# Attention units in stretches of two: regrouping a fused retention and feed-forward kernel

## The chip, the cores and the metric

The kernel runs on one core of a Trainium2 chip. A core has five engines that run beside each other and wait for each other by semaphores: TensorE (matmuls; the profile shows them as PE and the loading of weights as PEld), VectorE (DVE), ScalarE (ACT), GpSimd (POOL) and SyncE (SP), which here only issues DMAs. Matmul results land in PSUM, which the program divides into eight buffers of 128 partitions and 512 float32 columns. The metric is the device time of one execution in microseconds, as the median of several; lower is better.

## The reference

A retention layer (attention without softmax, with a decay for each head) is followed by a feed-forward layer with an ELU between its two products:

```python
B, H, S, D_ = q.shape                       # 8, 8, 576, 64
scores = (1 / sqrt(D_)) * q @ k^T
gamma = 1.0 - 2.0 ** (-5.0 - arange(H))
rel = pos[:, None] - pos[None, :]
Dmat = where(rel >= 0, gamma ** rel, 0.0)   # for each head
attn = (scores * Dmat) @ v
x = attn.transpose(0, 2, 1, 3).reshape(4608, 512)
h = x @ w_in                                # 512 x 2048
g = where(h > 0, h, exp(min(h, 0)) - 1)
out = g @ w_out                             # 2048 x 512, float32
```

## The kernel before, in words

**The decay as a scaling.** gamma^(i-j) is split into a factor on the rows of q and one on the rows of k (tiles `gq`, `gk`, `far_q`, `far_k`), so that a causal mask of ones and zeros is all that is left to do on the scores. Past chunks enter through a state, the sum of k^T v over the tokens before.

**Units.** Each batch has 512 tokens that are worked in blocks of 256 and a tail of 64. A *unit* is 256 tokens of one batch (half T = 0 or 1) for four heads (w = 0 or 1); eight batches give 32 units, numbered 0 to 31 in the order (batch, T, w). The tails of four batches form one tail item, t0 and t1 (numbers 32 and 33). For each unit q, k and v are loaded (`load_main`, line 380), scaled (`scaled`) and v is cast; q and k are then turned, by TensorE for units 0 to 6 and by a transpose DMA on SP from unit 7 on.

**Two forms.** A unit before `FAR` (line 211) is worked in two chunks of 128 tokens: it is loaded with one DMA for each of q, k and v, has one mask over 1024 columns, two running states (`mid`, `end`) and two block-diagonal copies of them (`s_mid`, `s_end`) for the matmuls. From `FAR` = 8 on, a unit is worked in four chunks of 64 tokens: two DMAs for each of q, k and v, half the columns in the scores and the mask, four running states and four block-diagonal copies. The running states are made by VectorE one after the other (`after_state` line 733, `after_far` line 789), the block-diagonal copies by POOL as a rule.

**A stretch.** TensorE does attention work in *stretches* (`stretch`, line 914). A stretch serves two units at once: the outputs of the one before (`do_inter`, old states times queries; `do_values`, masked scores times v) and the scores and the states of the present one (`do_scores`, `do_state`). The inter matmuls use the full array, those of scores, values and states work in quarters of it, 64 by 64. The scores go to the `sc` buffer (1024 columns), and the mask on VectorE makes `pt` of them. Outputs and states share two of the six PSUM buffers called `f`: columns 0 to 255 hold outputs, the rest states. ScalarE or VectorE copies the outputs to `xt`, two copies a unit (`put_x`, line 867). The tail items have scores, values and inter matmuls, but no states of their own.

**The feed-forward** fills TensorE between the stretches. The first product (`ffn1`, line 977) makes 512 columns in one `f` buffer from four matmuls; ScalarE takes the exponential (`e`), VectorE makes `em` (or ScalarE a relu in place) and the activation `g`. The second product (`ffn2`, line 1033) adds up 16 matmuls of 512 columns in an `f` buffer, in steps of four; ScalarE copies the result to `ot`, and SP writes it out, in one DMA for 128 rows or, where `HALVED` (line 217) names the block and its part, in two of 64 rows.

**What sets the order.** Nothing is ordered by hand. Every step is an `Op` with an engine, a cost, what it needs, the buffers that it takes and a rank, and `Plan.run` (line 68) plays the engines through with these costs and picks on each engine the step of lowest rank that can start. The instructions are then issued in this order, and on the chip each engine works through its own list in order. A changed cost, such as those of the tail loads (`load_tail`, line 426) and of their transposes (`prepare_tail`, line 567), thus changes the order, and so do a buffer's number of places in `SLOTS` (line 225: six `f`, one `sc`, two raw tail tiles `rqt`, eight `s_mid`). A stretch takes its `f` buffers through `reserve` (line 905).

Of the kernel before, what the change touches and what calls it, by code (L numbers as in the profile page):

```python
# [17 lines left out]
P = 128  # L18
# [192 lines left out]
FAR = 8  # L211
FAR_LD = 0.64
# [4 lines left out]
HALVED = ((10, 1), (10, 2), (12, 0), (12, 1), (12, 2))  # L217
# [16 lines left out]
def kernel(  # L234
# [191 lines left out]
    def load_tail(it):  # L426
# [140 lines left out]
    def prepare_tail(it):  # L567
# [3 lines left out]
        for m in range(2):  # L571
            for j in range(2):
# [14 lines left out]
                def emit_t(op, m=m, j=j):  # L587
# [5 lines left out]
                                     dma=(1.0, 32)))  # L593
# [24 lines left out]
    def far_pt(n):  # L618
        return tiles["pt", n].rearrange("p i h n -> p (i h n)")[:, : 8 * C].rearrange("p (x n) -> p x n", n=C)

    def do_scores(it):
        n = it.n
        sc = tiles["sc", n]
# [12 lines left out]
        if it.far:  # L636
            for x in range(4):
                for i in range(2):
                    r = slice(i * D, (i + 1) * D)
                    for c in range(2):  # L640
                        cs = slice(c * C, (c + 1) * C)
                        mm(sc[cs, i, x * C : (x + 1) * C], tt[r, 4 + x, cs], tt[r, x, cs], start=True, stop=True)
# [11 lines left out]
    def do_inter(it, xkey):  # L654
# [10 lines left out]
        if it.far:  # L665
            tt = tiles["qkT", n]
            for x in range(4):
# [4 lines left out]
                for hl in range(2):  # L672
                    acc((xkey, c), 0, 2, tiles[xkey, c][:, hl * P + e * C : hl * P + (e + 1) * C], s[:, hl],
# [11 lines left out]
    def do_values(it, xkey):  # L685
# [12 lines left out]
        vn, pt = tiles["vn", n], tiles["pt", n]  # L698
        if it.far:
            pt = far_pt(n)  # L700
            for hl in range(2):
                for e in range(2):
                    for c in range(2):
                        cs = slice(c * C, (c + 1) * C)
                        o = hl * P + e * C
                        for i in range(2):
                            acc((xkey, c), 0, i, tiles[xkey, c][i * D : (i + 1) * D, o : o + C], vn[cs, 2 * hl + i, e],
                                pt[cs, 4 * i + 2 * e + hl])
# [24 lines left out]
    def after_state(it, st, views, bank_keys):  # L733
# [3 lines left out]
        if it.far:  # L737
            return after_far(it, st, views, bank_keys, prev)

# [3 lines left out]
        def emit_mid(op):  # L743
            dst = tiles["mid", n]
            if prev is None:
                pin(copy[op.eng](dst, st_ap(0)))
            else:
                pin(nc.vector.tensor_tensor(dst, st_ap(0), tiles[prev[1]], ALU.add))

        mid = add(f"mid{n}", {"DVE": 0.29} if it.T else {"DVE": 0.29, "ACT": (0.3, 0.2)}, [st, prev and prev[0]],  # L750
                  emit_mid, it.rank + 2, take=[T("mid", ("mid", n), [P, 2, D], FP32)],
                  use=[views[0][0]] + ([prev[1]] if prev else []), banks=[bank_keys[0]])

        def emit_end(op):
            pin(nc.vector.tensor_tensor(tiles["end", n], st_ap(1), tiles["mid", n], ALU.add))

        end = add(f"end{n}", {"DVE": 0.29}, [mid], emit_end, it.rank + 3,
                  take=[T("end", ("end", n), [P, 2, D], FP32)], use=[views[1][0], ("mid", n)], banks=[bank_keys[1]])
        total[it.w] = (end, ("end", n))

        def block(src, key, name, dep):
            def emit(op):
                pin(alu[op.eng].tensor_tensor(
                    tiles[key].rearrange("p h (j d) -> p h j d", j=2),
                    tiles[src].unsqueeze(2).to_broadcast([P, 2, 2, D]),
# [23 lines left out]
    def after_far(it, st, views, bank_keys, prev):  # L789

        n = it.n
        it.bms = []
        for x in range(4):
# [4 lines left out]
            def emit(op, c=c, e=e, key=key, prev=prev):  # L798
                new = views[c][2]()[:, e * P : (e + 1) * P].rearrange("p (h d) -> p h d", h=2)
                if prev is None:  # L800
                    pin(copy[op.eng](tiles[key], new))
                else:
                    pin(nc.vector.tensor_tensor(tiles[key], new, tiles[prev[1]], ALU.add))  # L803

            run = add(f"{key[0]}{x}_{n}", {"DVE": 0.29} if prev else {"DVE": 0.29, "ACT": (0.3, 0.2)},
                      [st, prev and prev[0]], emit, it.rank + 2, take=[T(key[0], key, [P, 2, D], FP32)],
                      use=[views[c][0]] + ([prev[1]] if prev else []), banks=[bank_keys[c]])
            prev = run, key
            out = (name, it.b, it.T, it.w) + ((x + 1,) if x < 3 else ())

            def emit_b(op, key=key, out=out):
                pin(alu[op.eng].tensor_tensor(  # L812
                    tiles[out].rearrange("p h (j d) -> p h j d", j=2),
                    tiles[key].unsqueeze(2).to_broadcast([P, 2, 2, D]),
                    diag.unsqueeze(1).unsqueeze(3).to_broadcast([P, 2, 2, D]), ALU.mult,
                ))

            blk = add(f"b{x}_{n}", {"POOL": 0.62, "DVE": (0.42, 1.5)}, [run], emit_b, it.rank + 3,
                      take=[T(name, out, [P, 2, P], BF16)], use=[key])
            if x < 3:  # L820
                it.bms.append(blk)
            else:
                it.be = blk
        total[it.w] = prev

    def mask_step(it, sc):
        n = it.n
        def emit(op):
            if it.tail:
                pin(nc.vector.tensor_tensor(  # L830
                    tiles["pt", n].rearrange("p i h n -> p (i h n)").rearrange("p (x n) -> p x n", n=ST),
                    tiles["sc", n].rearrange("p i n -> p (i n)").rearrange("p (x n) -> p x n", n=ST),
# [3 lines left out]
            if it.far:  # L836
                pin(nc.vector.tensor_tensor(  # L837
                    far_pt(n).rearrange("p (i x) n -> p i x n", i=2),
                    tiles["sc", n][:, :, : 4 * C].rearrange("p i (x n) -> p i x n", n=C),
                    mask_t.unsqueeze(1).unsqueeze(2).to_broadcast([P, 2, 4, C]), ALU.mult,  # L840
# [4 lines left out]
                tiles["sc", n].rearrange("p i (h n) -> p (i h) n", h=2),  # L845
# [3 lines left out]
        it.mask = add(f"mask{n}", {"DVE": 0.69 if it.far else 1.22}, [sc], emit, it.rank + 1,  # L849
                      take=[T("pt", ("pt", n), [P, 2, 2, 2 * P], BF16)], use=[("sc", n)], banks=[("sc", 0)])  # L850
# [366 lines left out]
```

## Time and profile before

| | |
|---|---|
| median of 3 runs | 304.0 us (303.87 to 304.51) |
| the profiled execution | 305.64 us, span 303.9 us |
| granted TensorE clock | 1.00 throughout |
| busy: PE, DVE, ACT, POOL | 291.6, 214.2, 155.2, 178.4 us |
| DMA | 50.13 MB; the mean busy share of the 16 engines is 0.8 to 1.2 up to 200 us, 0.1 to 0.2 after 240 us |
| end of the last unit's attention / of the second tail | 218 us / 237 us, only feed-forward from then on |
| mean time of: exp on ACT, copy of 512 columns on ACT, g on DVE | 0.597, 0.587, 0.68 us |

The span runs from the first to the last instruction of the core; the execution's own time has some 1.7 us around it. In the rows that follow, "out<-in" names the tiles, a shape is partitions x elements, and a matmul's "64*64" or "128*128" is the part of the array that it uses. A timeline row gives start, length, engine, line and how many instructions it merges; in square brackets stands the idle time of the engine before it and what ended it. The length of a matmul's row has a modelled end, so distances between starts are the better measure.

### The profile page before, as it was taken

What the parts mean: (1) busy time and instruction counts of PE and PEld (TensorE: products, weight loads), DVE (VectorE), ACT (ScalarE), POOL (GpSimd) and SP (SyncE); (2) the same over time, 40 slices, a digit from 0 to 9 for tenths busy, and PEclk for the clock granted to TensorE, in tenths of its full rate; (3) what the DMA queues carried; (4) which work ended last, traced back from release to release, by engine and by line L of the source; (5) the groups of instructions that cost most, each with busy time, mean ns of one, the idle gap of its engine ahead of it and who ended that gap; (6) DMA issues with size and microseconds to landing.
All of it is one profiled execution on the core that took longest, in us unless ns stands there. A gap on an engine that the chain in (4) does not pass through costs nothing.

```text
span 303.9 us, 8654 instructions
## 1 busy us (share of the span) xinstructions
PE 291.6 (96%) x3378; PEld 169.6 (56%) x3418; DVE 214.2 (70%) x436; ACT 155.2 (51%) x305; POOL 178.4 (59%) x300
## 2 busy tenths in 40 slices
PE   8889999999999999999999999999997999999995
PEld 4768746767666754445554544545444544444444
DVE  5878935958877857996988897788871486666500
ACT  2439724748655546765855544445541583444311
POOL 5880389688989897889889889697532000000000
PEclk9999999999999999999999999999999999999999
DMA  7999998999899999989999999987667101011132
GB/s 206 270 206 210 235 303 218 173 218 187 194 193 232 214 185 204 206 193 183 193 188 224 204 186 199 204 169 171 137 130 168 37 2 36 35 36 37 43 97 71
DMA packets 142010, 50.13 MB, mean 165 GB/s; under 512 B 120720, under 2 KB 137488, under 8 KB 141968
## 3 DMA queue, kind: packets, MB, share of 16 engines
q1 hardware_dynamic: 137744, 45.37, 71.4%
q0 software_dynamic: 4224, 4.19, 8.3%
q8 instruction: 27, 0.44, 0.6%
q14 instruction: 15, 0.12, 0.1%
HBM read 36.70 MB, written 9.44 MB: 152 GB/s over the span
## 4 chain that ended last, share of the span: by engine, by line
PE 85%; DMA 6%; DVE 3%; issue 2%; SPq 1%; POOL 1%; ACT 1%; POOLq 0%; DVEq 0%; ACTq 0%
PE f L268 82%; PE sc L268 3%; DMA rv<-in_v_dram 3%; DMA rqk<-in_q_dram 2%; DMA rqt<-in_k_dram 1%; DVE em L1010 1%; DVE g L1020 1%; DMA qkTt<-qkt 1%; DVE g L1018 1%; SPq L404 1%; PE f L523 0%; ACT e L996 0%; POOL qkn L475 0%; POOL qkt L578 0%; DVE mid L803 0%
## 5 line engine op out<-in xcount | busy, mean ns | idle before, releaser
L268 PE MATMUL f<-xt,w_in_sb 128*128 128x256 bf16 (+1 forms) x755 | 139.8, 325 | 0.8 <-DVE xt L882 0.2
L268 PE MATMUL f<-w_out_sb,g 128*128 128x512 bf16 (+2 forms) x581 | 137.2, 367 | 3.4 <-issue 1.7
L996 ACT ACTIVATE e<-f 128x512 f32<-128x512 f32 x144 | 85.4, 597 | 77.7 <-PE f L268 73.5
L268 PEld LDWEIGHTS <-w_in_sb 128*128 128x128 bf16 x768 | 73.7, 98 | 52.0 <-DVE xt L882 0.5
L268 PEld LDWEIGHTS <-g 128*128 128x128 bf16 x608 | 56.5, 98 | 59.2 <-issue 1.0
L1010 DVE TENSOR_SCALAR em<-e 128x512 bf16<-128x512 f32 x88 | 49.2, 560 | 35.3 <-ACT e L996 34.7
L1020 DVE SCALAR_TENSOR_TENSOR g<-f,em 128x512 bf16<-128x512 f32 x88 | 60.4, 689 | 5.5 <-DVE em L1010 0.5
L812 POOL TENSOR_TENSOR s_mid<-mid,diag 128x256 bf16<-128x256 f32 x72 | 44.5, 630 | 15.1 <-DVE mid L803 9.5
L1018 DVE SCALAR_TENSOR_TENSOR g<-e,f 128x512 bf16<-128x512 f32 x56 | 37.6, 681 | 2.5 <-ACT f L1006 2.1
L1054 ACT COPY ot<-f 128x512 f32<-128x512 f32 (+2 forms) x37 | 20.8, 564 | 28.4 <-PE f L268 25.5
L475 POOL TENSOR_TENSOR qkn<-rqk,far_q 128x256 bf16<-128x256 f32 x48 | 31.0, 658 | 1.8 <-DMA rqk<-in_q_dram 1.6
L475 POOL TENSOR_TENSOR qkn<-rqk,far_k 128x256 bf16<-128x256 f32 x48 | 31.0, 660 | 0.0
L1006 ACT ACTIVATE f<-f 128x512 f32<-128x512 f32 x51 | 30.1, 594 | 0.0
L882 ACT CAST xt<-f 128x256 bf16<-128x256 f32 x52 | 18.1, 390 | 20.8 <-PE f L268 20.2
L510 POOL CAST vn<-rv 128x512 bf16<-128x512 f32 x28 | 18.2, 651 | 6.2 <-DMA rv<-in_v_dram 6.1
L837 DVE TENSOR_TENSOR pt<-sc,mask_t 128x512 bf16<-128x512 f32 x24 | 16.4, 681 | 5.9 <-PE sc L268 5.9
L803 DVE TENSOR_TENSOR mid<-f,mid 128x128 f32<-128x128 f32 x48 | 13.8, 288 | 3.5
L578 POOL TENSOR_TENSOR qkt<-rqt,gq 128x256 bf16<-128x256 f32 x16 | 10.1, 652 | 10.3 <-DMA rqt<-in_k_dram 10.2
L812 POOL TENSOR_TENSOR s_end<-end,diag 128x256 bf16<-128x256 f32 x24 | 15.6, 648 | 0.1
L475 POOL TENSOR_TENSOR qkn<-rqk,gq 128x256 bf16<-128x256 f32 x13 | 8.3, 648 | 12.0 <-DMA rqk<-in_q_dram 11.9
L843 DVE TENSOR_TENSOR pt<-sc,mask 128x1024 bf16<-128x1024 f32 x8 | 9.7, 1219 | 2.1 <-PE sc L268 2.0
L268 PE MATMUL sc<-qkT 64*64 64x64 bf16 (+1 forms) x512 | 11.0, 204 | 0.0
(83 smaller groups left out, 177.8 us busy)
## 6 DMA issues: line engine op xcount, KB each, us to landing
out_dram<-ot SPq DMA_DIRECT2D x26, 256.0 KB, 2.9
rqk<-in_q_dram SPq DMA_DIRECT2D x48, 128.0 KB, 3.4
rqk<-in_k_dram SPq DMA_DIRECT2D x48, 128.0 KB, 3.4
rv<-in_v_dram SPq DMA_DIRECT2D x48, 128.0 KB, 3.4
out_dram<-ot SPq DMA_DIRECT2D x19, 128.0 KB, 2.4
rqk<-in_q_dram SPq DMA_DIRECT2D x8, 256.0 KB, 6.1
rqk<-in_k_dram SPq DMA_DIRECT2D x8, 256.0 KB, 5.8
rv<-in_v_dram SPq DMA_DIRECT2D x8, 256.0 KB, 6.0
```

The source lines that it names most:

```text
L268: pin(nc.tensor.matmul(*a, **kw))
L475: pin(alu[op.eng].tensor_tensor(tiles[key][:, i, e], tiles[raw][:, :, e], g, ALU.mult))
L510: pin(copy[op.eng](tiles["vn", n], tiles["rv", n]))
L812: pin(alu[op.eng].tensor_tensor(tiles[out].rearrange("p h (j d) -> p h j d", j=2), tiles[key].unsqueeze(2).to_broadcast([P, 2, 2, D]), dia ...
L837: pin(nc.vector.tensor_tensor(far_pt(n).rearrange("p (i x) n -> p i x n", i=2), tiles["sc", n][:, :, : 4 * C].rearrange("p i (x n) -> p i ...
L882: pin(copy[op.eng](dst, src))
L996: pin(nc.scalar.activation(tiles[ekey], tiles[hkey], AF.Exp))
L1006: pin(nc.scalar.activation(ph, ph, AF.Relu))
L1010: pin(alu[op.eng].tensor_scalar_add(em, e, -1.0))
L1018: pin(nc.vector.scalar_tensor_tensor(g, e, -1.0, ph, ALU.add, ALU.min))
L1020: pin(nc.vector.scalar_tensor_tensor(g, ph, 0.0, tiles["em", blk, p], ALU.max, ALU.min))
L1054: pin(copy[op.eng](tiles[okey][:, :cols], tiles[pkey][:, :cols]))
```

## The change

Four things change.

- `FAR` goes from 8 to 12: units 8 to 11 are worked in the 128-token form, like the units before them.
- From unit 16 (`PAIR`) on, a stretch takes two units, those of the two head groups of the same batch and half. Their scores share one `sc` buffer and one mask; their states go to two `f` buffers of their own, so that one addition serves both units; their outputs fill two further `f` buffers, and one copy serves both units (`put_two`). The tiles of the running states become twice as wide.
- The planner's costs of the tail loads (issue 0.46 to 0.63, transfer 0.8 to 0.93) and of their transposes (1.0 to 1.3) are raised, and that of a 64-token load goes from 0.64 to 0.62.
- Only part (12, 1) of the output is still written in halves, where there were five parts.

In the order of instructions that results, TensorE has 32 groups of attention matmuls between feed-forward work where it had 40; SP issues 256 DMAs where it issued 272. Between the first and the second tail stretch stand 68 feed-forward matmuls of 512 columns where there were 60, and ahead of the first tail stretch 52 where there were 32.

```diff
-FAR = 8
-FAR_LD = 0.64
+PAIR = 16
+FAR = 12
+FAR_LD = 0.62
-HALVED = ((10, 1), (10, 2), (12, 0), (12, 1), (12, 2))
+HALVED = ((12, 1),)
...
-            chain[0] = add(name, {"SP": 0.46}, [], emit, len(plan.ops),
+            chain[0] = add(name, {"SP": 0.63}, [], emit, len(plan.ops),
...
-                           dma=(0.8, 32), after=chain.get(0))
+                           dma=(0.93, 32), after=chain.get(0))
...
-                                     dma=(1.0, 32)))
+                                     dma=(1.3, 32)))
...
+    def after_far(its, st, view, bank_keys):
+        b, t, n, m = its[0].b, its[0].T, its[0].n, len(its)
+        prev = total.get(its[0].w) if t else None
...
             def emit(op, c=c, e=e, key=key, prev=prev):
-                new = views[c][2]()[:, e * P : (e + 1) * P].rearrange("p (h d) -> p h d", h=2)
+                new, dst = view(c, e), tiles[key].rearrange("p w h d -> p w (h d)")[:, :m]
                 if prev is None:
-                    pin(copy[op.eng](tiles[key], new))
+                    pin(copy[op.eng](dst, new))
                 else:
-                    pin(nc.vector.tensor_tensor(tiles[key], new, tiles[prev[1]], ALU.add))
...
+                    pin(nc.vector.tensor_tensor(dst, new, tiles[prev[1]].rearrange("p w h d -> p w (h d)")[:, :m], ALU.add))
...
             if it.far:
+                w = 4 if it.two_of is None else 8
                 pin(nc.vector.tensor_tensor(
...
-                    mask_t.unsqueeze(1).unsqueeze(2).to_broadcast([P, 2, 4, C]), ALU.mult,
+                    mask_t.unsqueeze(1).unsqueeze(2).to_broadcast([P, 2, w, C]), ALU.mult,
...
+    def put_two(its, xkey, dep):
+        for c in range(2):
+            it = its[0]
+            def emit(op, c=c, it=it):
+                dst = tiles[it.xt][:, :, it.T * TB : (it.T + 1) * TB].rearrange("p h (e c r) -> p c h e r", e=2, c=2)[:, c]
+                pin(copy[op.eng](dst, tiles[xkey, c].rearrange("p (h e r) -> p h e r", e=2, r=C)))
...
-    def stretch(prev, it):
-        xkey = ("x", it.n if it else "last")
+    def stretch(prevs, its):
+        name = str(its[0].n) if its else "last"
+        apart = len(prevs) > 1 or len(its) > 1
+        xkey = ("x", name)
+        skey = ("s", name) if apart else xkey
...
         def emit(op):
-            if prev is not None:
-                do_inter(prev, xkey)
-            if it is not None:
+            for i, it in enumerate(prevs):
+                do_inter(it, xkey, *([i * 2 * P] if len(prevs) > 1 else []))
+            for it in its:
                 do_scores(it)
-            if prev is not None:
-                do_values(prev, xkey)
-            if it is not None and not it.tail:
-                do_state(it, views)
+            for i, it in enumerate(prevs):
+                do_values(it, xkey, *([i * 2 * P] if len(prevs) > 1 else []))
+            if states:
+                for it in its:
+                    do_state(it, view_of(it))
...
-        reserve(st, [(xkey, c) for c in range(2)])
+        reserve(st, ([(xkey, c) for c in range(2)] if prevs or not apart else []) +
+                ([(skey, c) for c in range(2)] if apart and states else []))
...
-    prev = None
-    for it in items[EARLY:]:
-        stretch(prev, it)
-        prev = it
-    stretch(prev, None)
+    prev, left = [], items[EARLY:]
+    while prev or left:
+        now = left[: 2 if left and left[0].far and left[0].n >= PAIR else 1]
+        left = left[len(now) :]
+        stretch(prev, now)
+        prev = now
```

More of the change, by code (lines that the diff above doesn't have):

```diff
@@ L808, in after_far @@
-            prev = run, key
[L809 to L824, printed above, removed]
+                    pin(nc.vector.tensor_tensor(dst, new, tiles[prev[1]].rearrange("p w h d -> p w (h d)")[:, :m], ALU.add))
+            t0 = 0.29 if m == 1 else 0.42
+            run = add(f"{key[0]}{x}_{n}", {"DVE": t0} if prev else {"DVE": t0, "ACT": (t0 + 0.02, 0.2)},
+                      [st, prev and prev[0]], emit, its[0].rank + 2, take=[T(key[0], key, [P, 2, 2, D], FP32)],
+                      use=[bank_keys[c]] + ([prev[1]] if prev else []), banks=[(bank_keys[c], 0)])
@@ new lines, in after_far, with emit_b @@
+            prev = run, key
+            for i, it in enumerate(its):
+                out = (name, b, t, it.w) + ((x + 1,) if x < 3 else ())
+                def emit_b(op, key=key, out=out, i=i):
+                    pin(alu[op.eng].tensor_tensor(
+                        tiles[out].rearrange("p h (j d) -> p h j d", j=2),
+                        tiles[key][:, i].unsqueeze(2).to_broadcast([P, 2, 2, D]),
+                        diag.unsqueeze(1).unsqueeze(3).to_broadcast([P, 2, 2, D]), ALU.mult,
+                    ))
+                blk = add(f"b{x}_{it.n}", {"POOL": 0.62, "DVE": (0.42, 1.5)}, [run], emit_b, it.rank + 3,
+                          take=[T(name, out, [P, 2, P], BF16)], use=[key])
+                if x < 3:
+                    it.bms.append(blk)
+                else:
+                    it.be = blk
@@ L929, in emit, with view_of @@
+        if its:
+            take.append(T("sc", its[0].sc, [P, 2, 512], FP32))
+        states = bool(its) and not its[0].tail
+        def view_of(it):
+            o = 0 if apart else 2 * P
+            o += it.w * 2 * P if len(its) > 1 else 0
+            return [((skey, c), 0, lambda c=c: tiles[skey, c][:, o : o + (2 * P if it.far else P)]) for c in range(2)]
         def emit(op):
-            if prev is not None:
-                do_inter(prev, xkey)
-            if it is not None:
+            for i, it in enumerate(prevs):
+                do_inter(it, xkey, *([i * 2 * P] if len(prevs) > 1 else []))
+            for it in its:
```

107 lines of the change are left out of this document (62 added, 45 removed).

## The prediction

> **What bounds the kernel now.** I read the page first, then the waits of TensorE, then its timeline around single attention stretches and around the waits, last the groups by shape. All durations come from the one profiled execution. It took 305.64 us, 1.7 us more than its span of 303.9; the median of the three plain runs is 304.0. I work out a change of the span and take it off the median.
>
> ```profile
> span 303.9 us, 8654 instructions
> PE 291.6 (96%) x3378; PEld 169.6 (56%) x3418; DVE 214.2 (70%) x436; ACT 155.2 (51%) x305; POOL 178.4 (59%) x300
> PE   8889999999999999999999999999997999999995
> PE 85%; DMA 6%; DVE 3%; issue 2%; SPq 1%; POOL 1%; ACT 1%; POOLq 0%; DVEq 0%; ACTq 0%
> ```
>
> TensorE is busy in nine tenths of every slice from the fourth on, except one (the 7, at 228 to 236 us), and 85% of the chain that ended last is its own work. A busy share alone proves little here, since the ends of matmuls are modelled. Their rate settles it: late in the run 49 matmuls of 512 columns stand in the chain as one piece of 10.74 us, 0.22 each, one behind the other. So each microsecond of TensorE's order counts, and each wait in it. After 23 us it waits for little:
>
> ```profile
> PE f L268 <- issue: 1.7, 11, 0.2
> PE sc L268 <- DMA qkTt<-qkt: 1.7, 1, 1.7
> PE f L268 <- DVE g L1020: 0.7, 1, 0.7
> ```
>
> The eleven "issue" waits are no time: at each of them 7 matmuls stand beside 8 weight loads, so a record is missing. Real are one wait of 1.73 us in the second tail stretch, for a transpose DMA, and one of 0.70 at 133 us, for VectorE. The other waits lie in the first 23 us, which the change leaves alone.
>
> What does a stretch cost? The first six lines are unit 7 in the 128-token form, the next five unit 10 in the 64-token form; I take the start of the first line to the start of the feed-forward matmul behind it.
>
> ```profile
> 58.69 0.27 PE L268 MATMUL f<-qkT,s_end 128*128 128x128 bf16 x2
> 58.80 0.28 PE L268 MATMUL f<-qkT,s_mid 128*128 128x128 bf16 x2
> 59.00 0.42 PE L268 MATMUL sc<-qkT 64*64 64x128 bf16 x16
> 59.25 0.39 PE L268 MATMUL f<-pt,vn 64*64 64x128 bf16 x16
> 59.47 0.29 PE L268 MATMUL f<-vn,qkn 64*64 64x64 bf16 x16
> 59.92 3.40 PE L268 MATMUL f<-w_out_sb,g 128*128 128x512 bf16 x15 [0.16 <-issue]
> ...
> 67.56 0.34 PE L268 MATMUL f<-qkT,s_mid 128*128 128x64 bf16 x6
> 67.83 0.32 PE L268 MATMUL sc<-qkT 64*64 64x64 bf16 x16
> 67.98 0.30 PE L268 MATMUL f<-pt,vn 64*64 64x64 bf16 x16
> 68.11 0.30 PE L268 MATMUL f<-vn,qkn 64*64 64x64 bf16 x16
> 68.34 0.39 PE L268 MATMUL f<-xt,w_in_sb 128*128 128x256 bf16 x2
> ```
>
> **Part 1: units 16 to 31 two at a time.** TensorE issues the same matmuls, in 8 stretches instead of 16. What a stretch costs beyond its matmuls shows in two places. The 16 score matmuls take 67.83 to 67.98 = 0.15, the 16 of the values 0.13, but the 16 of the state, which are of the same size, take 68.11 to 68.34 = 0.23 up to the next full-array matmul: 0.10 more. The six inter matmuls take 0.27; a stretch with eight takes 0.33 (80.44 to 80.77), so one costs 0.03, six cost 0.18, and 0.09 is left over ahead of the first 64-row matmul. The tail agrees: 16 inter matmuls took 236.44 to 237.00 = 0.56 = 16 x 0.03 + 0.08. So each passage from full array to quarters and back costs 0.19, and eight of them go: 8 x 0.19 = 1.52 us off TensorE's path. Were the 0.19 a cost per matmul after all, nothing would go: the ends are 0 and 1.52.
>
> The Trainium skill, "TensorEngine Tiling (Array Packing)", Key Properties, says that changing the tiling mode drains TensorE; the rows above agree, at 0.09 and 0.10 us. The Trainium skill, "TensorE: Matmul & The Clock Gate", Single matmul latency, gives a warm matmul a constant of some 166 ns beyond its columns; an estimate with two such drains a stretch is 8 x 0.33 = 2.7 us, and the sum below would be 300.2 by it. The rows decide for 0.19.
>
> The other engines win too, beside the path:
>
> ```profile
> L837 DVE TENSOR_TENSOR pt<-sc,mask_t 128x512 bf16<-128x512 f32 x24 | 16.4, 681 | 5.9 <-PE sc L268 5.9
> L803 DVE TENSOR_TENSOR mid<-f,mid 128x128 f32<-128x128 f32 x48 | 13.8, 288 | 3.5
> L830 DVE TENSOR_TENSOR pt<-sc,mask_t 128x1024 bf16<-128x1024 f32 x2 | 2.4, 1220 | 6.1 <-PE sc L268 6.1
> L777 DVE TENSOR_TENSOR s_mid<-f,diag 128x256 bf16<-128x256 f32 x2 | 0.8, 413 | 0.0
> ```
>
> Per pair VectorE has one mask of 1.22 for two of 0.68, and four additions of about 0.42 (nearest row: 256 columns read from f, 0.413) for eight of 0.29: 0.14 + 0.64 = 0.78 less, 6.2 over eight pairs. ScalarE has two copies of 0.588 for four of 0.390: 0.38 less a pair. None of it is on the path by itself.
>
> What it adds is pressure on f, the six PSUM buffers. A stretch took two of them, shared by outputs and states; a pair takes four, and two are left for the feed-forward, which fills one every 0.86 us (4 x 0.216) in its first product. The state buffers come free once mask and additions are through: 1.22 + 4 x 0.42 = 2.9 us after the stretch, against 0.68 + 4 x 0.29 = 1.8 before, with g steps of 0.69 between them. The matmul that then waits for a buffer holds up everything behind it on TensorE. Ends for one stretch: 0 (16 of the 17 stretches from unit 16 on are followed by no wait) and 0.70 (the one that VectorE made TensorE wait). The mean of these 17 is 0.04; with half as many buffers left I take twice that, 0.08, so 8 x 0.08 = 0.66 us.
>
> **Part 2: units 8 to 11 in the 128-token form.** With 8 inter matmuls the 64-token stretch costs 0.84 (80.44 to 81.28), with 6 it costs 0.78. The 128-token stretch costs 59.92 - 58.69 - 0.22 (the missing record) = 1.01, and without an earlier state 0.90 (48.20 to 49.10). Two units of each kind: 2 x 0.17 + 2 x 0.12 = 0.58 us more on TensorE. Beside the path: VectorE has four masks of 1.22 for 0.68 (+2.2) and 8 additions fewer (-2.3), even; POOL has 8 products of 0.63 fewer (-5.0); SP has 12 load issues fewer.
>
> **Part 3: the tails.** Only the planner's figures change, but the order does too: between the two tail stretches the feed-forward matmuls grow from 60 to 68, 8 x 0.216 = 1.73 us more time. On SP, five output issues stood between the last transpose of the first tail and that of the second, now two, since (10,1), (10,2) and (12,0) are no longer halved and one output moves behind: 3 x 0.55 (1.19 for two at 224.97) = 1.65. The first tail stretch does not eat this up: 52 feed-forward matmuls stand between the last pair and it, 32 stood there before, and tail loads on SP run ahead in that time. Together 3.4 us of room for a wait of 1.73:
>
> ```profile
> 231.57 0.63 PE L268 MATMUL f<-qkTt,s_end 128*128 128x64 bf16 x16
> 232.13 0.35 PE L268 MATMUL sc<-qkTt 64*64 64x64 bf16 x17
> 234.21 0.31 PE L268 MATMUL sc<-qkTt 64*64 64x64 bf16 x15 [1.73 <-DMA qkTt<-qkt]
> ```
>
> So -1.73, with 0 as the other end. Next late is the mask of that tail (1.22), which the last stretch awaits behind 8 matmuls (1.73): covered, as before. The wait of 0.70 at 133 us came while VectorE ran without a break from 126.5 on. Two pairs stand ahead of that point and take 2 x 0.78 off VectorE, more than the wait: -0.70, other end 0.
>
> **Sum.** -1.52 + 0.66 + 0.58 - 1.73 - 0.70 = -2.71: 304.0 - 2.7 = 301.3 us.
>
> **Rivals.** (a) The tail wait stays, because POOL's scaling and the slots of two raw tail tiles, not SP's issues, set the transposes. For it: POOL's tail scalings waited 10.2 us for their loads, in four places. Against it: 3.4 us of room. Price +1.73: 303.0. (b) The pair costs TensorE what its two units did, the 0.19 being no passage cost: +1.52, 302.8; the 16 tail inter matmuls speak against it. (c) Slower: the f buffers bind. If each pair stretch is followed by a wait for VectorE or ScalarE, the gain of 3.37 without such waits is gone at 3.37 / 8 = 0.42 us each; at 0.70 each it is +5.6, 306.2. For it: VectorE is 86% busy from 120 to 180 us, and only two buffers remain. Against it: the change takes work off VectorE and ScalarE there, and second-product groups hold a buffer for 3.5 us (16 x 0.216), so that two buffers feed TensorE for long. The Trainium skill, "TensorEngine Tiling (Array Packing)", PSUM Bottleneck, warns of just this, that packing speeds TensorE and not the emptying of PSUM; no row yet shows it here. (d) a and b together: 304.5, no change that can be told.
>
> **How the numbers follow.** Forecast 0.60, (a) 0.12, (b) 0.11, (c) 0.11, (d) 0.06. 0.2% (0.6 us) is about what a measurement of this kernel tells from no change. Faster: 0.60 + 0.12 + 0.11 = 0.83; same 0.06; slower 0.11. The low end takes the new waits at 0 and the sum at -3.37, and 0.3 more, since from start to start the two waits cost 1.87 and 0.87: 300.3. The high end takes in (a) and (b): 303.2. That leaves out 0.17.
>
> **What would show it.** In the profile after: eight stretches with 32 scores, each about 1.37 us long (two 0.78 less 0.19) or 1.49 with earlier states; units 8 to 11 at 0.9 to 1.0; no wait for qkTt; POOL some 5 and VectorE some 6 us less busy. The forecast fails if TensorE's waits list lines of xt, g or mid at several of the eight stretches, summing above 3 us, or if the wait for qkTt is still there.

## The result and the profile after

The changed kernel takes 302.44 us as the median of 10 executions (301.1 to 312.4), the kernel before 303.94 (303.39 to 305.75): a ratio of 0.9929, with an interval of 0.9903 to 0.9955, or 2.2 us less (1.4 to 2.9). Ratios, here and below, compare means and leave out executions more than 1.5% above the fastest of their kernel; medians and ranges take in all. Run twice more on two other occasions the changed kernel took 302.06 and 302.25, with ratios of 0.993 and 0.9928. The forecast was 301.3, in a range of 300.3 to 303.2: the sign and the range hold, and by the ratio the gain came out about a fifth smaller than the 2.7 us of the sum.

The first profile taken of the changed kernel (span 309.5 us) shows an execution in which one VectorE instruction stood for 10 us; it is read further down. What is compared with the profile before is therefore a profile of the same kernel run again (`e0_again`, 303.26 us, span 301.6). Its page:

```profile
span 301.6 us, 8544 instructions
PE 295.5 (98%) x3402; PEld 170.3 (56%) x3402; DVE 212.6 (70%) x390; ACT 152.1 (50%) x287; POOL 174.2 (58%) x292
PE   8899999999999999999999999999999999999996
PE 88%; DVE 4%; DMA 4%; POOL 2%; ACT 0%; issue 0%; SPq 0%; ACTq 0%; DVEq 0%
```

The slice that was a 7, at 228 to 236 us, is a 9 now. TensorE's "busy" went up, from 291.6 to 295.5 us, in a shorter run: fewer records are missing, which is one more reason to go by starts. Its waits:

```profile
PE f L269 <- DVE zero L274: 1.3, 1, 1.3
PE f L524 <- DVE qkn L476: 0.6, 1, 0.6
PE f L269 <- DVE vn L511: 0.4, 1, 0.4
PE sc L269 <- DVE qkT L530: 0.2, 1, 0.2
PE f L269 <- DVE xt L907: 0.2, 1, 0.2
PE f L269 <- DVE pt L851: 0.2, 1, 0.2
```

All of them lie in the first 24 us. The wait for qkTt (1.7) and the one for g at 133 us (0.7) are gone, and none came in their place. A stretch of two units (units 18 and 19, with the outputs of 16 and 17), then the second tail stretch:

```profile
125.54 0.51 PE L269 MATMUL f<-qkT,s_mid 128*128 128x64 bf16 x12
125.98 0.45 PE L269 MATMUL sc<-qkT 64*64 64x64 bf16 x32
126.26 0.44 PE L269 MATMUL f<-pt,vn 64*64 64x64 bf16 x32
126.52 0.52 PE L269 MATMUL f<-vn,qkn 64*64 64x64 bf16 x32
126.97 0.60 PE L269 MATMUL f<-xt,w_in_sb 128*128 128x512 bf16 x2
...
230.72 0.63 PE L269 MATMUL f<-qkTt,s_end 128*128 128x64 bf16 x16
231.28 0.45 PE L269 MATMUL sc<-qkTt 64*64 64x64 bf16 x32
231.55 0.44 PE L269 MATMUL f<-pt,vt 64*64 64x64 bf16 x32
231.92 0.82 PE L269 MATMUL f<-w_out_sb,g 128*128 128x512 bf16 x3
```

From start to start the stretch of two takes 125.54 to 126.97 = 1.43 us, and the second tail 230.72 to 231.92 = 1.20, where it took 3.15 before. On VectorE, groups with their shapes kept apart (count, busy us, mean ns, idle before):

```profile
L1059 DVE TENSOR_SCALAR em<-e 128x512 bf16<-128x512 f32 x96 | 52.0, 543 | 39.3 <-ACT e L1045 38.7
L845 DVE TENSOR_TENSOR pt<-sc,mask_t 128x1024 bf16<-128x1024 f32 x8 | 9.8, 1220 | 2.1 <-PE sc L269 2.1
L807 DVE TENSOR_TENSOR mid<-f,mid 128x256 f32<-128x256 f32 x16 | 6.8, 425 | 1.8
```

The merged mask takes 1.22 us and the merged addition 0.425, as the sum had them (1.22 and 0.42). em stands 96 times, where it stood 88 times before: the planner gave VectorE eight more of them.

How executions differ has to be said once, since it limits every reading by the span. In the start-up, TensorE begins its steady feed-forward work at 22.63 us in the profile before and at 20.8 to 23.5 us in those of the runs that follow. What comes after that point varies less (two profiles of the changed kernel with spans of 301.6 and 299.9 us have 278.47 and 278.03 behind it), so I give it beside the times as "the rest": 281.31 us before, 278.47 in the run above.

### The profile page after: what moved, and what is told of

Its sections match the earlier page's. It is cut to its first block, busy times and chain, and to the rows that moved or that the text cites. A ratio compares the mean times of both kernels' runs of the same rounds, so it can differ in the third digit from the quotient of the medians.

```text
span 309.5 us, 8509 instructions
## 1 busy us (share of the span) xinstructions
PE 293.9 (95%) x3367; PEld 170.4 (55%) x3402; DVE 219.5 (71%) x390; ACT 152.2 (49%) x287; POOL 173.2 (56%) x292
## 4 chain that ended last, share of the span: by engine, by line
PE 89%; DVE 4%; SPq 2%; DMA 2%; issue 1%; POOL 1%; ACT 0%; ACTq 0%; DVEq 0%
PE f L269 86%; DVE em L1059 3%; PE sc L269 3%; SPq L405 2%; DMA rqk<-in_q_dram 2%; POOL qkn L476 1%; PE f L524 1%; POOL w_in_sb L454 0%; DVE g L1069 0%; ACT e L1045 0%; DVE xt L907 0%; ACT ot L1103 0%; ACTq L1103 0%; DVEq L1069 0%
## 5 line engine op out<-in xcount | busy, mean ns | idle before, releaser
L1059 DVE TENSOR_SCALAR em<-e 128x512 bf16<-128x512 f32 x96 | 60.4, 632 | 40.7 <-ACT e L1045 40.1
L1069 DVE SCALAR_TENSOR_TENSOR g<-f,em 128x512 bf16<-128x512 f32 x96 | 65.7, 689 | 5.7
L1067 DVE SCALAR_TENSOR_TENSOR g<-e,f 128x512 bf16<-128x512 f32 x48 | 32.1, 680 | 4.3 <-ACT f L1055 4.1
L476 POOL TENSOR_TENSOR qkn<-rqk,far_q 128x256 bf16<-128x256 f32 x40 | 26.1, 669 | 3.1 <-DMA rqk<-in_q_dram 3.1
L476 POOL TENSOR_TENSOR qkn<-rqk,far_k 128x256 bf16<-128x256 f32 x40 | 25.9, 663 | 0.0
L851 DVE TENSOR_TENSOR pt<-sc,mask 128x1024 bf16<-128x1024 f32 x12 | 14.6, 1217 | 4.3 <-PE sc L269 4.2
L907 ACT CAST xt<-f 128x256 bf16<-128x256 f32 x25 | 9.6, 428 | 14.7 <-PE f L269 14.6
L476 POOL TENSOR_TENSOR qkn<-rqk,gk 128x256 bf16<-128x256 f32 x22 | 13.4, 624 | 2.5 <-DMA rqk<-in_k_dram 2.4
L883 ACT CAST xt<-f 128x512 bf16<-128x512 f32 x16 | 8.6, 589 | 11.6 <-PE f L269 11.6
L845 DVE TENSOR_TENSOR pt<-sc,mask_t 128x1024 bf16<-128x1024 f32 (+1 forms) x12 | 12.5, 1038 | 2.2 <-PE sc L269 2.1
```

Of the source, the lines that this page charges most:

```text
L476: pin(alu[op.eng].tensor_tensor(tiles[key][:, i, e], tiles[raw][:, :, e], g, ALU.mult))
L845: pin(nc.vector.tensor_tensor(tiles[it.pt].rearrange("p i h n -> p (i h n)")[:, : 2 * w * C].rearrange("p (i x n) -> p i x n", i=2, n=C), ...
L851: pin(nc.vector.tensor_tensor(tiles["pt", n].rearrange("p i h n -> p (i h) n"), tiles[it.sc].rearrange("p i (h n) -> p (i h) n", h=2), mas ...
L1059: pin(alu[op.eng].tensor_scalar_add(em, e, -1.0))
L1067: pin(nc.vector.scalar_tensor_tensor(g, e, -1.0, ph, ALU.add, ALU.min))
L1069: pin(nc.vector.scalar_tensor_tensor(g, ph, 0.0, tiles["em", blk, p], ALU.max, ALU.min))
```

## The experiments

The first four ran on one chip beside 31 executions of the kernel before (median 304.29).

**The change again, and each part undone.**

> The changed kernel once more, on the same chip as its variants. The theory of the prediction: 301 to 302.5 us, eight pair stretches of 1.37 or 1.49 us on TensorE, no wait of TensorE for qkTt, none for VectorE above 0.7 us, and the em step of VectorE at about 51 us, which took 10.0 us in the execution profiled first while GpSimd worked without a break, at most 1 us. The rival theory, that GpSimd's unbroken work from 50 us on is a standing cost of the change: em steps between 50 and 62 us of 2 us and more in this execution too, and a wait of TensorE for g behind them.

302.06 us, ratio 0.993 (0.9886 to 0.9974). No em took more than 0.91 us in its profile, so the em of 10 us is no standing cost of the change.

```diff
-FAR = 12
+FAR = 8
```

> Part 2 undone: units 8 to 11 in the 64-token form again, the pairs and the tails kept. The theory of the prediction, in which these units only cost TensorE 0.58 us: 0.6 us faster than the changed kernel of this call. The rival, in which the 128-token form pays by what it takes off GpSimd (8 products of 0.63 us, 5.0 in all) and SP (12 loads): 0.5 to 2 us slower than the changed kernel, with waits of TensorE for units 16 and later that the changed kernel does not have.

Part 2 undone: 304.22 us, ratio 0.9992 (0.9964 to 1.002). Almost the whole gain is gone: by the means that the ratios compare, this kernel is 1.7 us slower than the changed one beside it (interval 0.5 to 2.9). It is not because TensorE has more matmuls: the stretches of units 8 to 11 are shorter, as expected. Waits of TensorE came back:

```profile
PE f L269 <- DVE g L1069: 0.9, 1, 0.9
PE f L269 <- DVE g L1067: 0.4, 1, 0.4
```

Its timeline shows both in the second stretch of two:

```profile
128.69 0.51 PE L269 MATMUL f<-qkT,s_mid 128*128 128x64 bf16 x12
129.13 0.44 PE L269 MATMUL sc<-qkT 64*64 64x64 bf16 x32
129.41 0.44 PE L269 MATMUL f<-pt,vn 64*64 64x64 bf16 x32
129.89 0.22 PE L269 MATMUL f<-vn,qkn 64*64 64x64 bf16 x2
130.49 0.44 PE L269 MATMUL f<-vn,qkn 64*64 64x64 bf16 x30 [0.38 <-DVE g L1067]
131.79 1.46 PE L269 MATMUL f<-xt,w_in_sb 128*128 128x512 bf16 x6 [0.86 <-DVE g L1069]
```

This stretch takes 3.10 us in place of 1.43. The state matmuls wait in the midst of it for an `f` buffer that a g step must free, and the feed-forward behind it waits for another. That is rival (c) of the prediction, in one place, and what the Trainium skill, "TensorEngine Tiling (Array Packing)", PSUM Bottleneck, warns of. The rest is 280.23 us, 1.8 more than with part 2.

What stands ahead of that stretch differs too. The first line is this run, the next two are the last of the row in `e0_again`, where second and first products take turns from 117.8 to 125.5 us:

```profile
117.38 11.47 PE L269 MATMUL f<-xt,w_in_sb 128*128 128x512 bf16 x52
...
123.81 1.03 PE L269 MATMUL f<-xt,w_in_sb 128*128 128x512 bf16 x4
124.68 1.03 PE L269 MATMUL f<-w_out_sb,g 128*128 128x512 bf16 x4
```

With part 2 undone the stretch comes right behind 52 matmuls of the first product in a row, each four of which fill an `f` buffer that ScalarE and VectorE must empty. The planner orders everything anew when the form of four units changes. Whether the waits come from that order or from the form of the units, no run here separates.

```diff
-PAIR = 16
+PAIR = 99
```

> Part 1 undone: no stretch of two, units 8 to 11 and the tails as changed. The theory of the prediction: TensorE pays eight passages of 0.19 us again, 1.5 us, and is rid of the waits for f buffers, so 0.9 to 1.5 us slower than the changed kernel of this call. The rival, that a pair costs TensorE what its two units did: no slower, and the stretches of 0.78 and 0.84 us add up to what the pair stretches take.

Part 1 undone: 303.33 us, ratio 0.9962 (0.9932 to 0.9991). By the means this is 1.0 us over the whole change, with an interval (-0.1 to 2.2) that takes in no difference; the rest is 278.78 us, 0.3 and 0.8 more than in the two profiles of the changed kernel. The traces are clearer: the 17 single stretches from unit 16 on take 13.74 us from start to start, the nine that take their place in `e0_again` 13.02. There is no wait for qkTt, and none for g behind the first 24 us.

```diff
-HALVED = ((12, 1),)
+HALVED = ((10, 1), (10, 2), (12, 0), (12, 1), (12, 2))
...
-            chain[0] = add(name, {"SP": 0.63}, [], emit, len(plan.ops),
+            chain[0] = add(name, {"SP": 0.46}, [], emit, len(plan.ops),
...
-                           dma=(0.93, 32), after=chain.get(0))
+                           dma=(0.8, 32), after=chain.get(0))
...
-                                     dma=(1.3, 32)))
+                                     dma=(1.0, 32)))
```

> Part 3 undone: the planner's old costs of tail loads and tail transposes and the five halved outputs, pairs and units 8 to 11 as changed. The theory of the prediction: the second tail stretch waits again for qkTt, by 1 to 3 us, and the kernel is slower than the changed one by about that. The rival, that the wait went with the shift of the tails by the pairs: no wait for qkTt above 0.3 us and the time of the changed kernel within 0.5 us.

Part 3 undone: 302.31 us, ratio 0.9945 (0.9918 to 0.9972). The second tail stretch takes 1.20 us and waits for nothing. The rival holds: with parts 1 and 2 in place the tail wait does not need part 3 to go.

**Part 3 alone.** Is it at least enough by itself? The kernel before with these figures reversed; this kernel, the next two and the one with em on ScalarE (302.34 us) ran beside 21 executions of the kernel before (median 304.64).

> The kernel before with part 3 alone: the planner's figures of the tail loads and transposes (0.63, 0.93, 1.3) and the one halved output. In the kernel after with part 3 undone the wait for qkTt did not come back (its second tail stretch took 1.20 us, against 3.15 in the kernel before), so part 3 is not needed once parts 1 and 2 are in. Theory A: it is sufficient all the same, as the prediction's room of 3.4 us says: no wait of TensorE for qkTt, second tail stretch about 1.2 us, 1.7 us less than before (ratio 0.9944). Theory B: the wait went with the other parts and part 3 does nothing for it: the wait of 1.5 to 1.9 us stays, ratio within 0.998 to 1.002.

303.88 us, ratio 0.9971 (0.994 to 1.0003). The wait is gone: theory A has the mechanism, at about half the amount. The first of the kernel's waits of TensorE:

```profile
PE f L268 <- DVE zero L273: 1.3, 1, 1.3
PE f L268 <- ACT vn L510: 0.8, 1, 0.8
PE f L268 <- DVE g L1020: 0.7, 1, 0.7
```

and the timeline of its second tail stretch, 238.38 to 239.59 = 1.21 us:

```profile
238.38 0.63 PE L268 MATMUL f<-qkTt,s_end 128*128 128x64 bf16 x16
238.94 0.45 PE L268 MATMUL sc<-qkTt 64*64 64x64 bf16 x32
239.22 0.44 PE L268 MATMUL f<-pt,vt 64*64 64x64 bf16 x32
239.59 0.60 PE L268 MATMUL f<-w_out_sb,g 128*128 128x512 bf16 x2
```

The rest falls by 2.01 us (281.31 to 279.30), but the ratio is worth 0.9 us, anywhere from 1.8 less to 0.1 more. Part 3 removes the wait of the profiled execution; whether the median execution of the kernel before waits as long there, no trace shows. It took 1.64 us less than the profiled one (304.0 against 305.64).

**The order within a stretch of two.** In the stretch shown above the 32 scores take 0.28 us, the 32 values 0.26, but the 32 states, up to the next full-array matmul, 0.45, in other stretches 0.43 to 0.58. Is it the states, or the last place?

```diff
+            if states and len(its) > 1:
+                for it in its:
+                    do_state(it, view_of(it))
             for it in its:
                 do_scores(it)
             for i, it in enumerate(prevs):
                 do_values(it, xkey, *([i * 2 * P] if len(prevs) > 1 else []))
-            if states:
+            if states and len(its) == 1:
```

> The kernel after with one order changed: in the stretches of two units the 32 state matmuls stand ahead of the 32 scores and the 32 values, not behind them. In the kernel after the scores take 0.28 us, the values 0.26 and the states, last, 0.42 to 0.58 up to the next full-array matmul. Theory of the count: the small matmuls slow down after some 60 in a row, whichever they are. Then the states, first, take 0.26 to 0.30, the values, last, 0.42 to 0.58, the stretch is as long as before (1.40 to 1.65), and the time is within 0.6 us of the kernel after. Rival: the state matmuls themselves are slow when 32 follow one another; then they take 0.42 or more in the first place too, and the values 0.36 with the passage back. Second rival: the masks, whose scores now end 0.26 us later, make TensorE wait at the next steps: over 0.6 us slower.

The timeline of the stretch that answers to the one shown above:

```profile
125.42 0.51 PE L269 MATMUL f<-qkT,s_mid 128*128 128x64 bf16 x12
125.86 0.45 PE L269 MATMUL f<-vn,qkn 64*64 64x64 bf16 x32
126.14 0.44 PE L269 MATMUL sc<-qkT 64*64 64x64 bf16 x32
126.39 0.45 PE L269 MATMUL f<-pt,vn 64*64 64x64 bf16 x32
126.77 1.47 PE L269 MATMUL f<-xt,w_in_sb 128*128 128x512 bf16 x6
```

The states, first now, take 0.28 us, the scores 0.25, and the values, last, 0.38. So it is not the state matmuls as such, which rules out the first rival. But it is not the last place alone either, as the theory of the count has it: in the seven stretches with 32 values last these take 0.38 to 0.41 in five, little more than the 0.36 of their pace with the passage back, and 0.52 and 0.59 in two. States are slow where they stand last; why is open. The stretch is shorter, against the theory: the same one takes 1.35 in place of 1.43, the nine together 12.62 in place of 13.02. And the kernel is not slower, which rules out the second rival: 301.24 us, ratio 0.9888 (0.9857 to 0.9919), which lies below that of the changed kernel though the intervals overlap. The rest is 277.59 us, 0.9 less than in `e0_again`, and the 0.4 us of the stretches are about half of that.

**A held instruction.** The first profile of the changed kernel had this among the waits of TensorE:

```profile
PE f L269 <- DVE g L1069: 8.0, 1, 8.0
```

The timelines of VectorE and, for three of its instructions, of GpSimd show where:

```profile
51.06 10.02 DVE L1059 TENSOR_SCALAR em<-e 128x512 bf16<-128x512 f32 x1 [1.85 <-ACT e L1045]
61.18 0.69 DVE L1069 SCALAR_TENSOR_TENSOR g<-f,em 128x512 bf16<-128x512 f32 x1
...
50.53 0.61 POOL L476 TENSOR_TENSOR qkn<-rqk,gk 128x256 bf16<-128x256 f32 x1
51.10 0.61 POOL L476 TENSOR_TENSOR qkn<-rqk,gq 128x256 bf16<-128x256 f32 x1
51.65 0.61 POOL L511 CAST vn<-rv 128x512 bf16<-128x512 f32 x1
```

An em, 0.42 us by itself and up to 0.93 beside GpSimd, stood for 10.02 us, to the end of a row in which GpSimd started one instruction after the other without a break; TensorE waited 8.0 us for the g behind it. That row lasts 20.5 us at this place in the changed kernel (36 instructions), 11.4 before (19). Of the two other long executions (312.4 and 311.51 us), and of the longest of the kernel before (up to 309.89), no trace shows the cause. To test it, 72 products whose result nobody uses are added on GpSimd at a place where it has run out of work and VectorE still makes em:

```diff
+    def emit_jam(op):
+        pin(nc.gpsimd.memset(jin, 1.0))
+        for j in range(72):
+            pin(nc.gpsimd.tensor_tensor(jout[:, j % 12], jin, far_q[:, 0, :4].unsqueeze(2).to_broadcast([P, 4, D]), ALU.mult))
+
+    add("jam", {"POOL": 72 * 0.57 + 0.3}, [o for o in plan.ops if o.name == "ex_T_3"], emit_jam, 10 ** 6)
```

> The kernel after with 72 further products on GpSimd, whose result nobody uses, from about 237 us on, some 40 us or more without a break, beside the em instructions of the blocks T and 14 on VectorE, which otherwise run with GpSimd idle. Theory of the held instruction: a VectorE em can be kept for as long as GpSimd goes on without a break. Then some executions are 10 to 40 us longer (above 312 us), and in such a profile an em of 10 to 40 us stands in that stretch. Rival: the two engines take turns, each em is at most 1 us long, TensorE does not wait, and the median is within 1 us of the kernel after with no more executions above 306 us than it has.

329.93 us (328.73 to 331.35, 6 executions), ratio 1.0837. Each of them is long, which is more than the theory said. The added row began at 222.5 us, earlier than the expected 237. The largest wait of TensorE in that profile:

```profile
PE f L269 <- DVE g L1069: 25.6, 1, 25.6
```

Two em in the timeline of VectorE, and the added row in that of GpSimd:

```profile
225.10 0.84 DVE L1059 TENSOR_SCALAR em<-e 128x512 bf16<-128x512 f32 x1 [0.26 <-ACT e L1045]
235.90 28.43 DVE L1059 TENSOR_SCALAR em<-e 128x512 bf16<-128x512 f32 x1 [2.58 <-ACT e L1045]
...
222.53 41.51 POOL L1204 TENSOR_TENSOR jout<-jin,far_q 128x256 bf16<-128x256 bf16 x72
```

One em came through in 0.84 us, a later one stood for 28.43, until 264.33; GpSimd's row ended at 264.04. The control keeps the 72 products and makes em of these two blocks on ScalarE:

```diff
-        md = add(f"md_{blk}_{p}", {"ACT": 0.6, "DVE": 0.66 if first else 0.54}, [ex], emit_m, rank,
+        md = add(f"md_{blk}_{p}", {"ACT": 0.6} if blk in ("T", 14) else {"ACT": 0.6, "DVE": 0.66 if first else 0.54}, [ex], emit_m, rank,
```

> The same 72 needless products on GpSimd as in the run that took 329.9 us, but em of the blocks T and 14 on ScalarE, so that no em stands beside the unbroken run. Theory of the held instruction: no VectorE instruction is held, TensorE does not wait, 302 to 303 us. Rival: the unbroken run of GpSimd stops VectorE whatever it does (mask, g, additions); then a wait of 20 us or more is there again and the time is above 320.

301.28 us, ratio 0.9899 (0.9829 to 0.9969, two executions). Three em of an earlier block still stand at the start of the row; they come through in 0.48 to 0.88 us. Beside the same row of GpSimd (its last 66 instructions at 224.53, 38.06 us long), VectorE's g, which reads PSUM, went on at its usual pace between 222 and 262 us (groups of VectorE in that window):

```profile
L1067 DVE SCALAR_TENSOR_TENSOR g<-e,f 128x512 bf16<-128x512 f32 x19 | 12.7, 686 | 15.2 <-ACT f L1055 15.2
L1069 DVE SCALAR_TENSOR_TENSOR g<-f,em 128x512 bf16<-128x512 f32 x4 | 2.8, 691 | 0.4
```

So it is em that is held, not VectorE as a whole: instructions that read PSUM go on. The Trainium skill, "SBUF — State Buffer", section Who interferes with whom, says that VectorE's second pair of SBUF ports is GpSimd's, that a `tensor_scalar` in its two-port mode takes it, and that whoever comes first has it for the whole instruction while the other fully blocks. The runs agree that em is held and g is not. They go further in the length: the em was kept out not for one GpSimd instruction of 0.6 us, but for all that followed without a break. Why some em come through and others do not is open.

**Without em beside GpSimd.** The same step on ScalarE for all blocks but the first two, T and 14:

> The kernel after, but the step that makes em on VectorE is done on ScalarE for all feed-forward blocks except the first two, the block T and block 14, which come when GpSimd has run out of work. Theory of the held instruction: in one execution of the kernel after an em of VectorE stood for 10.02 us while GpSimd ran 18 instructions without a break. With no em beside GpSimd, no execution above 306 us, where the kernel after had 2 of 10 at 311 to 312. The median: VectorE loses about 86 instructions of 0.42 us or more (36 us) and ScalarE gains as many of 0.6 (52 us, from 155 to some 207 us busy), both under 70%, so 301 to 302.5, as the kernel after or up to 1 us better. Rival: ScalarE, which must then do e and f for each group in order, comes too late for TensorE in places: waits for ScalarE of 0.3 us or more at several stretches, 303 to 306.

302.34 us (301.69 to 304.59), ratio 0.9935 (0.9905 to 0.9966). No execution above 304.6, and the median is that of the changed kernel. ScalarE bears it; no wait for it shows. Ten executions without a long one prove little when the changed kernel has long ones in about 3 of 30. With the two further kernels below that have em on ScalarE there are 29, none above 304.8, which speaks for the theory without proving it.

**Is it VectorE that part 2 relieves?** Part 2 undone, and em on ScalarE as in the run above; this kernel, the two after it and the control above (301.28 us) ran beside 24 executions of the kernel before (median 303.90).

> Units 8 to 11 back in the 64-token form (part 2 undone) and em on ScalarE, except in the first two feed-forward blocks, the block T and block 14. With part 2 undone alone TensorE waited 2.6 us for VectorE at 128 to 158 us and the time was 304.22, where the kernel after has 302.06. Theory: VectorE was late there, because em took 0.65 us in place of 0.42 beside a busy GpSimd, and the f buffers that it frees came late. Without em on VectorE these waits are gone, and the kernel gains the 0.55 us that the 128-token form costs TensorE: 301.5 to 302.0 (the kernel after without em took 302.34). Rival: the buffers themselves are too few for eight more additions; waits of 1 us or more stay at 128 to 158 us, and the time stays at 303.5 to 304.5.

302.74 us, ratio 0.9967 (0.9938 to 0.9995): between the two bands. The 2.6 us of waits in the expectation are too many: with part 2 undone alone TensorE's waits after start-up sum to 1.5 us, 0.9 and 0.4 at the stretch shown and 0.2 at 159 us. The stretch that took 3.10 us takes 2.57 (128.80 to 131.37); again it comes right behind a row of first-product matmuls, 54 of them. Busy us from 120 to 130 us, in the order PE, PEld, DVE, ACT, POOL (then clock, DMA share and GB/s), first with part 2 undone alone:

```profile
120.00:130.00 10.00, 9.95 (x120) 5.05 (x118) 9.86 (x17) 9.10 (x18) 10.00 (x16) 1.00 1.00 204
```

and with em on ScalarE as well:

```profile
120.00:130.00 10.00, 9.67 (x117) 4.80 (x117) 6.43 (x10) 10.00 (x22) 8.67 (x16) 1.00 1.00 212
```

The changed kernel, with part 2, has more room around its own second stretch of two:

```profile
118.00:128.00 10.00, 10.00 (x149) 5.23 (x148) 8.63 (x15) 5.20 (x9) 8.58 (x14) 1.00 0.86 189
```

With part 2 undone VectorE has no gap and ScalarE hardly one; with em moved ScalarE has none. Work on one of them moved to the other, and the place stayed late. My theory that VectorE alone was too slow falls; by these rows both together are short there, behind a long row of first-product matmuls and with the states of a pair at once. No run changes that order alone.

**Both, and the change once more.**

> State matmuls first in the stretches of two, and em on ScalarE except in the first two blocks, T and 14. If the two gains add up, 0.8 us under the kernel after for the order, 0 to 0.5 us for em: 300.8 to 301.5, with no execution above 305. If what the order won was VectorE's (states freed 0.5 us earlier), the two are the same gain: 301.2 to 302.0.

> The kernel after once more, on the same chip as the other three, to compare with: 302.0 to 302.5 us, ratio 0.993, some execution above 306 us.

States first and em on ScalarE: 301.39 us (300.91 to 302.28), ratio 0.9908 (0.9874 to 0.9943). The change itself beside it: 302.25 (301.23 to 311.51), ratio 0.9928 (0.9893 to 0.9962). 301.39 lies in both bands of the expectation and does not decide between them. By the means the two changes together are worth 0.6 us beside the changed kernel (interval 0.0 to 1.2), just clear of no difference. The rest after start-up is 277.41 against 278.03; with the order alone it was 277.59, so em adds little to the order. The ratios against the kernel before overlap.

## Why the prediction was right, and where not

**The pairs (-1.52): right mechanism, mis-sized.** The step that failed is "each passage from full array to quarters and back costs 0.19, and eight of them go". Nine stretches took 13.02 us in `e0_again`, 17 took 13.74 with part 1 undone: 0.72 went, half of it. The passages did go: the inter, score and value matmuls of a pair take about what the rows before said (0.44, 0.275, 0.26). But I priced 96 small matmuls in a row by rows of 48, and the states at their end are slower: 0.43 to 0.58 up to the next full-array matmul, where 32 at the pace of the others and one passage back would take 0.26 + 0.10 = 0.36. By the means the part is worth 1.0 us, with an interval that takes in none, and by the rest 0.3 to 0.8, so the stretches are the better measure. In these rows rival (b), that nothing is saved, does not hold, and neither do the 2.7 us that I estimated by the Trainium skill, "TensorE: Matmul & The Clock Gate", Single matmul latency.

**Waits for the f buffers (+0.66): not there, and the risk was real.** `e0_again` has none at the eight stretches. But with part 2 undone they are there, 1.7 us in a single stretch. The mean over 17 single stretches was no measure for this: in the two traces that have such a wait, the pair stands behind more than 50 first-product matmuls in a row.

**Units 8 to 11 (+0.58): right on TensorE, wrong for the kernel.** The six stretches from unit 7 to unit 12 took 5.18 us in the profile before, with 0.22 for each missing record as in the prediction, and 5.77 in `e0_again`: +0.59. (The rows that the prediction calls unit 10 hold the scores of unit 9; nothing rests on the name.) Yet undoing the part makes the kernel 1.7 us slower. The step that failed is "beside the path": "even" for VectorE is a count over the kernel as a whole, and says nothing of how far VectorE and ScalarE lag when the first pairs come, nor of the order that the planner makes of the feed-forward there. With part 2 undone both engines are almost without a gap at that place and the f buffers bind; with it they do not. By what steps units 8 to 11, at 65 to 78 us, bring that about at 120 is open.

**The tail wait (-1.73): gone, for a reason that was only half right.** Part 3 does remove it alone; so do parts 1 and 2 without part 3. And the amount was that of a profiled execution 1.64 us above the median: alone, the ratio makes 0.9 us of it. Rival (a) is out.

**The wait at 133 us (-0.70): gone, but not for the reason given.** The prediction has two pairs take more than the wait off VectorE. With part 1 undone there are no pairs, and the wait is gone all the same. With part 2 undone the pairs are there, and TensorE waits 0.9 and 0.4 us for g at about that place. With part 3 alone it stays (0.7). As far as these runs tell, it goes with part 2, to which the prediction gave no such effect.

**The sum.** In the traces TensorE loses 2.84 us after start-up: 0.75 in the stretches from unit 16 on (13.77 to 13.02), 1.95 in the tail, 0.87 at 133 us, 0.45 at the end behind the last matmul, less 0.59 for units 8 to 11 and 0.6 of small differences elsewhere. The ratios of the three comparisons give some 2.1 us, their medians 1.5 to 2.2. That the total came out so near is in part luck. Two errors of opposite sign, the pairs (0.80 too much) and the new waits (0.66 too much), nearly cancelled, and the division among the parts is wrong: taken back one at a time, the part that was to cost 0.58 us comes out largest (1.7), then the pairs (1.0 or less), and part 3 does nothing that can be told (0.2). Why the traces lose more than the ratios give is not shown; the profiled execution before took 1.64 us more than the median, which would explain it.

**What would show it.** Units 8 to 11 stand at 1.01, 0.90, 0.90, 1.01 (said: 0.9 to 1.0) and no wait for qkTt is left, as said. The stretches of two take 1.40 to 1.65 between the first and the tail (said: 1.37 or 1.49). GpSimd is 4.2 us less busy (said: 5), VectorE 1.6 (said: 6), where the planner put eight more em on it, some 4.3 us at 0.543 each.

## What to carry to other kernels

Price a group of small matmuls at the length that it will have, and try which of its groups stands last. Where a planner orders the work, a change of form in one place moves the work in others: a form that cost TensorE 0.6 us came with a kernel that was 1.7 us faster. So look at the engines that free the buffers stretch by stretch, at both of them together, and at what stands ahead of each burst. And take the price of a wait from several executions, not from one profile.

## What the runs showed of the hardware

- A VectorE `tensor_scalar` from float32 to bfloat16 in SBUF can be held for as long as GpSimd issues without a break: 10.02 us once, 28.43 us with a longer row, where it takes 0.42 alone. VectorE instructions that read PSUM ran on at 0.69 beside such a row.
- In the changed kernel the 64-by-64 matmuls with 64 columns behind a full-array piece start 8.1 to 8.6 ns apart (32 in 0.26 to 0.275 us). As the last 32 ahead of a full-array matmul, 32 values take 0.37 us behind 32 others (second tail stretch) and mostly 0.38 to 0.41 behind 64 (states first); 32 states take 0.43 to 0.58 in that place and 0.274 in the first. What makes the difference no run shows.
